# Attention scores in four array quarters, values loaded in wider runs, sums from the exponential, and a hint for a far branch

## The chip, the cores and the metric

The kernel runs on one core of a Trainium2 chip. The metric is the device time of one launch in microseconds; lower is better. One execution of each kernel is profiled as well. The engines are named as in the profile: PE is TensorE (PEld its weight loads), DVE VectorE, ACT ScalarE, POOL GpSimd, and SP the engine that issues most of the transfers. A `q` behind a name is that engine's sequencer.

## The reference

Three stages follow each other: attention over local windows plus block summaries, a mixture of eight experts with one expert per token, and a dense feed-forward layer with ELU.

```python
B, H, S, D = 2, 8, 768, 64
k_sum = k.reshape(B, H, nb, 32, D).max(axis=3)
v_sum = v.reshape(B, H, nb, 32, D).mean(axis=3)
scores_l = where(|i - j| < 16, scale * q @ k.T, -1e9)
scores_s = scale * q @ k_sum.T + log(32)
a = exp(scores_all - max);  a = a / (sum(a) + 1e-9)
x = a @ concat(v, v_sum)                          # (1536, 512) tokens
...
expert = argmax(x @ w_gate);  gate = softmax(...)[expert]
x = gate * (relu(x @ w1[expert]) @ w2[expert])    # 8 experts, 512 -> 1024 -> 512
...
h = x @ w_in;  out = elu(h) @ w_out               # 512 -> 2048 -> 512
```

## The kernel before

**Tiling of the attention.** The eight heads of a batch entry are taken as four pairs, so there are eight pairs in all. A pair holds 128 channels (two heads of 64) on the partitions. The 768 positions are 24 blocks of 32, of which two neighbouring ones make a query block of 64; a query block sees a window of 96 keys and 24 block summaries, 120 columns (`NK`). Four query blocks make a group; there are 24 groups, three for each pair.

**Steps of a group.** `scores(g)` (token `s:g`) multiplies queries by keys into a PSUM tile `sc` (L879): for each of the four query blocks two matmuls, one for each head, over all 128 partitions. So that a head's queries meet only its own keys, the query tile holds every head apart with zeros in the other head's rows; `zero_q` (L695, L696) writes these zeros and `queries` (L772) copies each head's rows. DVE then adds the mask and takes the row's extreme (L884, with a read of its accumulator after each of the four), and ACT takes the exponential (L888). `turn_weights(g)` (`t:g`) transposes the four tiles on PE into `pt` (L895), and ACT copies them to `pts` (L897). `average(g)` (`a:g`) multiplies by the values into `av` (L909), whose rows in SBUF carry a column of ones beside the values, so that one column of `av` is the sum of the weights; DVE adds 1e-9 (L915, twice), takes the reciprocal (L916) and scales into `xo` (L917).

**Other steps of a pair.** `load_k`, `load_q` and `load_v` (`lk`, `lq`, `lv`) issue loads on SP's queue. `key_sums` (`ks`, L807) takes the block maxima, `keys` (`kw`, L819 to L836) writes windows and summaries into one tile, and `sum_and_place_values` (`vq`, L855 to L860) forms the means of the values on PE, copies them on ACT and stores them into the value tile by a small transfer. `x_transpose` (`T`) and `x_store` (`X`) pass the finished tokens on to the routing.

**What sets the order.** The string `PROGRAM` lists these steps by hand; each engine executes its instructions in the order in which the steps issue them. Semaphores are placed by a tile framework: a PSUM pool with two buffers (`ps_a` for `sc`, `ps_b` for `av` and `pt`) makes a group wait for the group two before it.

**After the attention.** Everything from the routing on needs tokens of all groups: gather, five slots of 256 tokens, one wider slot, the dense layer. Behind the fifth slot an `If` (L1216, `extra`) holds spare slots which these inputs don't need; all engines branch over it. The wide slot's first layer (`hw`, L983 to L985, with ACT and DVE at L1160 and L1161) runs partly ahead of this branch and partly behind it.

Of the kernel before, what the change touches and what calls it, by code (L numbers as in the profile page):

```python
# [22 lines left out]
P = 128  # L23
# [9 lines left out]
VO = 2  # L33
VW = VO + 2 * D + VO
# [17 lines left out]
lq s:0 qp:0:v:1:3 zero:3 lv:0 ones:1 lk:1 lv:1 ks:1 vq:0:y  # L52
s:1 lv:2 kw:1:g:v lk:2 lk:3 t:0
s:2
s:3 t:1 a:0 t:2 zero:2
s:5 ks:2 vq:1:y kw:2 ones:3
s:4 a:1 a:2 t:5 t:3 ones:2 ks:3 lk:4 t:4 lv:3 vq:2:c kw:3 a:3
s:6
s:7 lv:4 a:4 a:5 t:6
s:8 t:7 consts lk:5  # L60
s:9 a:6 vq:3:c lv:5 t:8 T:1:0:c ks:4
s:10 kw:4 t:9
s:11 a:8 T:0:0 a:7 t:10 a:9 ks:5 lk:6 lv:6 t:11 T:0:1:c kw:5 ks:6 vq:4:c lk:7
# [50 lines left out]
def attention_moe_elu_kernel(  # L114
# [563 lines left out]
    pa = actx.enter_context(tc.tile_pool(name="ps_a", bufs=2, space=PSUM))  # L678

# [14 lines left out]
    def zero_q(n, eng):  # L694
        eng.memset(q_sb[n][D:P, :, 0, :], 0.0)  # L695
        eng.memset(q_sb[n][0:D, :, 1, :], 0.0)  # L696

    def ones_of(n):
        for col in (VO - 1, VO + 2 * D):
            nc.gpsimd.memset(v_sb[n][:NK, :, col], 1.0)  # L700

    def prep_consts():
        nc.scalar.activation(exps[:, 0, :], ident[:, 0:E], AF.Exp)
        zero_q(0, nc.vector)
        nc.gpsimd.memset(mask[:, :, 0:WIN], 0.0)
        nc.gpsimd.memset(mask[:, :, WIN:], 8.0 * LOG_BLOCK)
        for h in range(2):
            m = mask[h * D:(h + 1) * D, :, 0:WIN]
            for sgn in (1, -1):
                nc.gpsimd.affine_select(  # L710
                    out=m, in_=m, pattern=[[sgn * HALO, 3], [-sgn, WIN]], compare_op=ALU.is_ge,
                    fill=NEG, base=REACH, channel_multiplier=sgn,
                )
        nc.gpsimd.memset(sel, 0.0)
# [7 lines left out]
        ones_of(0)  # L722
# [62 lines left out]
    def load_v(n):  # L785
        if n >= B * NPAIR:
            return
        b, pr = divmod(n, NPAIR)
        sl = n % NQ
        vv = v_sb[sl][:, :, VO:VO + 2 * D]  # L790
        vb = v[b, :, pr * 2 * D:(pr + 1) * 2 * D]
        nc.sync.dma_start(
            out=vv[0:WIN, 1:NBLK - 1, :],
            in_=bass.AP(vb.tensor, vb.offset + win_start(1) * DM, [[DM, WIN], [QB * DM, NBLK - 2], [1, 2 * D]]),
# [3 lines left out]
            in_=bass.AP(vb.tensor, vb.offset, [[DM, WIN], [win_start(NBLK - 1) * DM, 2], [1, 2 * D]]),  # L798
# [71 lines left out]
    def scores(g):  # L870
        n, i0 = order[g]
        sl = n % NQ
        sc = pa.tile([P, 4, P], F32, tag="sc", name="sc")
        t = wk.tile([P, 4, NK], F32, tag="t", name="t", bufs=2)
        pe = wk.tile([P, 4, NK], F32, tag="pe", name="pe")
        nm = wk.tile([P, 4], F32, tag="nm", name="nm")
# [4 lines left out]
        for u in range(4):  # L881
            i = i0 + u
            kind = 0 if i == 0 else 2 if i == NBLK - 1 else 1
            nc.vector.tensor_tensor_reduce(  # L884
                out=t[:, u, :], in0=sc[:, u, :NK], in1=mask[:, kind, :], scale=-0.125, scalar=3.0e38,
                op0=ALU.add, op1=ALU.min, accum_out=nm[:, u:u + 1],
            )
            nc.scalar.activation(pe[:, u, :], t[:, u, :], AF.Exp, bias=nm[:, u:u + 1], scale=-1.0)  # L888
        st[g] = pe

    def turn_weights(g):
        pe = st[g]
        pt = pb.tile([P, 4, P], F32, tag="pt", name="pt")
        for u in range(4):
            nc.tensor.transpose(pt[:NK, u, :], pe[:, u, :], ident)  # L895
        pts = wk.tile([P, 4, P], F32, tag="pts", name="pts", bufs=2)
        nc.scalar.activation(pts[:NK], pt[:NK], AF.Copy)  # L897
        st[g] = pts

    def average(g):  # L900
        n, i0 = order[g]
        b, pr = divmod(n, NPAIR)
        pts = st.pop(g)
        av = pb.tile([P, 4, P], F32, tag="av", name="av")
        for u in range(4):
            for h in range(2):
                hs = slice(h * D, (h + 1) * D)
                col = VO - 1 + h * D
                nc.tensor.matmul(av[hs, u, :D + 2], pts[:NK, u, hs], v_sb[n % NQ][:NK, i0 + u, col:col + D + 2],  # L909
                                 start=True, stop=True)  # L910

        r = wk.tile([P, 4], F32, tag="r", name="r")
        for h in range(2):
            hs = slice(h * D, (h + 1) * D)
            nc.vector.tensor_scalar_add(r[hs], av[hs, :, h * (D + 1)], 1e-9)  # L915
        nc.vector.reciprocal(r, r)  # L916
        nc.vector.tensor_tensor(  # L917
            out=xo[b][:, i0:i0 + 4, pr, :], in0=av[:, :, 1:D + 1], in1=r.unsqueeze(2).to_broadcast([P, 4, D]),
            op=ALU.mult,
        )  # L920

    def x_transpose(ch, hf, e="c"):

        b, lo = divmod(4 * ch, NBLK)
        if ch not in xts:
            xts[ch] = rt2.tile([P, 2, 2, 4, QB], F32, tag="xts", name="xts")
        xt = pa.tile([P, 2, 4, QB], F32, tag="xt", name="xt")
        for bl in range(4):
            nc.tensor.transpose(
                xt[:, :, bl, :],  # L930
                xo[b][:, lo + bl, 2 * hf:2 * hf + 2, :].rearrange("p a d -> p (a d)"),
                ident,
            )
        copy[e](xts[ch][:, hf].rearrange("p a b q -> p a (b q)"), xt.rearrange("p a b q -> p a (b q)"))

    def x_store(ch):
        b, lo = divmod(4 * ch, NBLK)
        for par in range(2):
            nc.sync.dma_start(
                out=x_dram[4 * ch * QB:4 * (ch + 1) * QB, par * 256:(par + 1) * 256].rearrange(  # L940
                    "(i q) f -> q i f", q=QB),
                in_=xo[b][par * D:(par + 1) * D, lo:lo + 4].rearrange("q i a d -> q i (a d)"),
            )
# [109 lines left out]
    with tc.manual_schedule():  # L1053
# [6 lines left out]
        zero_q(1, nc.gpsimd)  # L1060
# [335 lines left out]
```

## Time and profile before

| | us |
|---|---|
| median of 3 runs | 549.58 |
| lowest to highest | 549.4 to 552.67 |
| profiled execution, its own time | 553.14 |
| its span, first to last instruction | 551.4 |
| PE busy in the span | 512.5 |
| DVE busy | 354.6 |
| ACT busy | 238.2 |
| POOL busy | 168.7 |

The span leaves 1.74 us of the profiled execution outside. Durations and waits below come from this one execution, which was 3.56 us above the median of the runs. A busy engine is not yet a bound: shares are averages over stages with different limits.

### The profile page before, as it was taken

To read this page: it belongs to the slowest core of one execution; us is meant where nothing else is said; L and a number is where in the kernel's file an instruction comes from. 1 tells how busy PE (TensorE), PEld (TensorE's weight loads), DVE (VectorE), ACT (ScalarE), POOL (GpSimd) and SP (SyncE) were. 2 spreads that over 40 slices of the span, in tenths; PEclk is the share of its full clock that TensorE was granted. 3 is DMA by queue.
4 is the path that set the end of the run, shared out by engine and by line. 5 is a ranking of instruction groups with operands and counts; after the bars stand their busy time and mean duration, and the time that the engine had idled before them with its cause. 6 is when DMAs were issued, how large, how long until landed. Compare 5 with 4: busy or idle time off the path is not lost.

```text
span 551.4 us, 9535 instructions
## 1 busy us (share of the span) xinstructions
PE 512.5 (93%) x3605; PEld 443.1 (80%) x3605; DVE 354.6 (64%) x820; ACT 238.2 (43%) x444; POOL 168.7 (31%) x164
## 2 busy tenths in 40 slices
PE   6798998889999996979987999999999999999995
PEld 4686786779999996979965888888888888888884
DVE  5766788868869785538998778774334354434342
ACT  3644567434555545433444434353323243323231
POOL 6556504633345373503345224322000001100002
PEclk7987999989999999889999999999999999999999
DMA  8788726746666577752545434101000000100001
GB/s 199 205 179 224 172 35 231 226 151 215 223 214 181 203 260 224 226 159 76 162 144 153 114 85 134 51 0 58 19 0 1 0 1 38 40 1 1 0 1 76
DMA packets 34999, 64.56 MB, mean 117 GB/s; under 512 B 3136, under 2 KB 18112, under 8 KB 34944
## 3 DMA queue, kind: packets, MB, share of 16 engines
q1 hardware_dynamic: 31384, 56.57, 35.1%
q0 software_dynamic: 2000, 6.56, 3.3%
q10 hardware_dynamic: 1560, 0.74, 0.9%
q8 instruction: 31, 0.51, 0.4%
q14 instruction: 24, 0.20, 0.1%
HBM read 56.38 MB, written 6.29 MB: 114 GB/s over the span
## 4 chain that ended last, share of the span: by engine, by line
PE 47%; DVE 6%; issue 2%; POOL 1%; POOLq 0%; ACT 0%; DVEq 0%
PE o L985 7%; PE o L983 7%; PE o L984 7%; PE hp L984 7%; PE hp L983 7%; PE hp L985 7%; DVE v L215 2%; PE hw L983 1%; PE hw L985 1%; PE hw L984 1%; DVE v L212 1%; DVE raw L218 1%; DVE x L212 1%; POOL out_dram L1313 1%; DVE h_lo L1037 0%
## 5 line engine op out<-in xcount | busy, mean ns | idle before, releaser
L1271 DVE SCALAR_TENSOR_TENSOR xs<-xs,xs 128x512 f32<-128x512 f32 x48 | 33.2, 691 | 82.0 <-ACT xs L1268 82.0
L984 PE MATMUL hp<-h_lo,whi 128*128 128x512 f32 x192 | 75.1, 391 | 0.0
L983 PE MATMUL hp<-h_hi,whi 128*128 128x512 f32 x192 | 75.0, 391 | 0.0
L985 PE MATMUL hp<-h_hi,wlo 128*128 128x512 f32 x192 | 75.0, 390 | 0.0
L224 POOL TENSOR_TENSOR wlo<-raw,whi 128x512 fp32r<-128x512 f32 x32 | 45.4, 1425 | 96.5 <-ACT whi L223 96.5
L983 PE MATMUL o<-whi,x_hi 128*128 128x512 f32 x168 | 65.8, 391 | 1.7 <-ACT x_hi L1282 1.7
L985 PE MATMUL o<-whi,x_lo 128*128 128x512 f32 x168 | 65.8, 392 | 0.9 <-DVE x_lo L1284 0.9
L1267 ACT ACTIVATE xs<-hp 128x512 f32<-128x512 f32 x48 | 28.6, 596 | 87.9 <-PE hp L985 87.9
L984 PE MATMUL o<-wlo,x_hi 128*128 128x512 f32 x168 | 65.7, 391 | 0.0
L1313 POOL DMA_INDIRECT out_dram<-x,idx_cmp x12 | 11.6, 968 | 172.6 <-DVE x L1312 156.7
L296 ACT ACTIVATE whi<-raw 128x1024 fp32r<-128x1024 f32 x46 | 48.0, 1054 | 24.5 <-DMA raw<-in_w_dram 24.1
L299 DVE TENSOR_TENSOR wlo<-raw,whi 128x1024 fp32r<-128x1024 f32 x32 | 43.9, 1379 | 19.1 <-ACT whi L296 19.0
L983 PE MATMUL hp<-x_hi,whi 128*128 128x256 f32 x160 | 47.0, 294 | 4.0 <-DVE h_lo L1003 3.9
L1282 ACT ACTIVATE x_hi<-xs 128x512 fp32r<-128x512 f32 x42 | 26.6, 632 | 54.2 <-DVE xs L1273 54.2
L299 POOL TENSOR_TENSOR wlo<-raw,whi 128x1024 fp32r<-128x1024 f32 x14 | 35.5, 2538 | 47.3 <-ACT whi L296 47.3
L984 PE MATMUL yp<-h_lo,whi 128*128 128x256 f32 x160 | 46.3, 290 | 2.3 <-DVE h_lo L1003 2.2
L1284 DVE TENSOR_TENSOR x_lo<-xs,x_hi 128x512 fp32r<-128x512 f32 x40 | 30.3, 758 | 28.1 <-ACT x_hi L1282 27.3
L984 PE MATMUL hp<-x_lo,whi 128*128 128x256 f32 x160 | 46.5, 291 | 1.1 <-DVE x_lo L979 1.1
L985 PE MATMUL yp<-h_hi,wlo 128*128 128x256 f32 x160 | 46.1, 288 | 0.7 <-DVE wlo L299 0.7
L983 PE MATMUL yp<-h_hi,whi 128*128 128x256 f32 x160 | 46.8, 292 | 0.0
L985 PE MATMUL hp<-x_hi,wlo 128*128 128x256 f32 x160 | 46.3, 289 | 0.0
L983 PEld LDWEIGHTS hp<-h_hi,whi 128*128 128x128 f32 x192 | 36.0, 188 | 7.9
(252 smaller groups left out, 1184.1 us busy)
## 6 DMA issues: line engine op xcount, KB each, us to landing
raw<-in_w_dram SPq DMA_DIRECT2D x48, 512.0 KB, 4.6
raw<-in_win_dram SPq DMA_DIRECT2D x16, 512.0 KB, 4.1
raw<-in_wout_dram SPq DMA_DIRECT2D x16, 512.0 KB, 3.7
v<-in_v_dram SPq DMA_DIRECT2D x8, 480.0 KB, 6.9
x_dram<-xo SPq DMA_DIRECT2D x12, 256.0 KB, 4.9
kr<-in_kT_dram SPq DMA_DIRECT2D x7, 384.0 KB, 3.8
qr<-in_qT_dram SPq DMA_DIRECT2D x7, 384.0 KB, 4.3
v<-in_v_dram SPq DMA_DIRECT2D x8, 96.0 KB
```

Source lines behind the costliest of these rows:

```text
L212: nc.vector.tensor_scalar(out=v, in0=top, scalar1=3, scalar2=0x3FFFFFF8, op0=ALU.logical_shift_left, op1=ALU.bitwise_and)
L224: nc.gpsimd.tensor_tensor(out=wlo[n][:, k, :], in0=w, in1=as_f32(whi[n][:, k, :]), op=ALU.subtract)
L296: nc.scalar.activation(part, raw, AF.Copy)
L299: eng_.tensor_tensor(out=wlo[n][:, k, :], in0=raw, in1=as_f32(part), op=ALU.subtract)
L983: nc.tensor.matmul(o, a_hi, b_hi, start=first, stop=False)
L984: nc.tensor.matmul(o, a_hi, b_lo, start=False, stop=False)
L985: nc.tensor.matmul(o, a_lo, b_hi, start=False, stop=last)
L1267: nc.scalar.activation(u, hp, AF.Exp)
L1271: nc.vector.scalar_tensor_tensor(out=u, in0=u, scalar=1.0, in1=t, op0=ALU.add, op1=ALU.mult)
L1282: nc.scalar.activation(gh, g, AF.Copy)
L1284: (nc.gpsimd if twice else nc.vector).tensor_tensor(out=gl, in0=g, in1=as_f32(gh), op=ALU.subtract)
L1313: puts.append(nc.gpsimd.indirect_dma_start(out=out[:, :], out_offset=bass.IndirectOffsetOnAxis(ap=idx_cmp[:, 4 * blk + t:4 * blk + t + 1], ...
```

## The change

- **Scores.** The query tile has no zeros. Each matmul takes 64 partitions (one head) into 64 output partitions (one query block of 64), and four of them, one after the other, address the four quarters of the array: head 0 into the upper half, head 1 into the lower, then crosswise. Two neighbouring query blocks lie side by side on the partitions, and the two heads in two different banks.
- **PSUM.** The score tile is one tile `sc` of three banks by two sides, allocated once; a group takes the halves `2*(g % 3)` and the next. `av` is one tile of one bank with two sides.
- **Values.** Two pairs' values share one tile. Pairs 0 and 1 are loaded apart; from pair 2 on one load brings two pairs, in runs of 1 KB (512 bytes before). The tokens `lv:3`, `lv:5` and `lv:7` are gone, `lv:4` and `lv:6` stand elsewhere. The columns of ones are gone.
- **Sums.** The exponential on ACT writes the row's sum through its accumulator; DVE adds 1e-9 once.
- **Stores.** `x_store` issues one transfer for each chunk, not two.
- **Hint.** The branch over the spare slots has a prefetch hint, "likely taken", on all five engines.

```diff
@@ PROGRAM
-lq s:0 qp:0:v:1:3 zero:3 lv:0 ones:1 lk:1 lv:1 ks:1 vq:0:y
+lq s:0 qp:0:v:1:3 lv:0 lk:1 lv:1 ks:1 vq:0:y
...
-s:4 a:1 a:2 t:5 t:3 ones:2 ks:3 lk:4 t:4 lv:3 vq:2:c kw:3 a:3
+s:4 a:1 a:2 t:5 t:3 ks:3 lk:4 t:4 vq:2:c kw:3 a:3
@@ PSUM
+    av_of = ...tile_pool(name="ps_v", bufs=1, space=PSUM)).tile([P, 2, 2, 2, D], F32, name="av")
...
+    sc_of = psc.tile([P, 3, 2, 2, P], F32, name="sc")
@@ load_v
+        w = 2 * D if n < 2 else 4 * D
+        vv = values(n) if n < 2 else v_sb[n // 2 % (NQ // 2)]
@@ scores
-        for u in range(4):
-            for h in range(2):
-                nc.tensor.matmul(sc[h * D:(h + 1) * D, u, :NK], q_sb[sl][:, i0 // 4, h, u * QB:(u + 1) * QB],
-                                 k_sb[sl][:, i0 + u, :], start=True, stop=True)
+        half_of = [divmod(2 * (g % 3) + h, 3) for h in range(2)]
+        sc = [sc_of[:, bank, side] for side, bank in half_of]
...
+        for u in range(2):
+            for p, h in ((0, 0), (1, 1), (1, 0), (0, 1)):
+                i, hs = i0 + 2 * u + p, slice(h * D, (h + 1) * D)
+                nc.tensor.matmul(sc[h][p * QB:(p + 1) * QB, u, :NK], q_sb[sl][hs, i, :], k_sb[sl][hs, i, :],
+                                 start=True, stop=True)
...
-            nc.scalar.activation(pe[:, u, :], t[:, u, :], AF.Exp, bias=nm[:, u:u + 1], scale=-1.0)
+                nc.scalar.activation(pe[:, u, h, :], t[:, u, h, :], AF.Exp, bias=nm[:, u, h:h + 1], scale=-1.0,
+                                     accum_out=sums[:, u, h:h + 1])
@@ average
-        av = pb.tile([P, 4, P], F32, tag="av", name="av")
+        av = av_of[:, g % 2]
...
-        for h in range(2):
-            hs = slice(h * D, (h + 1) * D)
-            nc.vector.tensor_scalar_add(r[hs], av[hs, :, h * (D + 1)], 1e-9)
+        nc.vector.tensor_scalar_add(r, sums, 1e-9)
@@ around the spare slots
+                if j + 1 == SURE:
+                    tc.mark_branch_hint_location("spare", hint="LikelyTaken", engines=[...])
...
-                with tc.If(nslots > j):
+                with tc.If(nslots > j, label="spare" if j == SURE else None):
```

The first place is PE from the scores of group 5 to the transposes after `a:2`, with the semaphores on which each row waits (the number behind a name tells one buffer of a tile from another). Before:

```order
L879 MATMUL sc_394<-k1_132,q1_128 64x120 [waits DVE_49,PE_49]
L879 MATMUL sc_394<-k1_132,q1_128 64x120 x7
L855 MATMUL pv_416<-v1_136,sel_142 64x128 [waits DMAHW1_49]
L855 MATMUL pv_416<-v1_136,sel_142 64x128 [waits DMAHW0_49]
L855 MATMUL pv_416<-v1_136,sel_142 64x128 x10
L879 MATMUL sc_440<-k1_132,q1_128 64x120 [waits DVE_49,PE_49]
L879 MATMUL sc_440<-k1_132,q1_128 64x120 x7
L909 MATMUL av_460<-v0_135,pts_369 64x66 [waits Activation_49]
L909 MATMUL av_460<-v0_135,pts_369 64x66 x7
L909 MATMUL av_474<-v0_135,pts_390 64x66 [waits DVE_49,Activation_49]
L909 MATMUL av_474<-v0_135,pts_390 64x66 x7
L895 MATMUL pt_488<-ident_61,pe_396 120x128 [waits Activation_49] x4
```

The same place on PE after the change:

```order
L881 MATMUL sc_122<-k1_140,q1_136 64x120 [waits DVE_49]
L881 MATMUL sc_122<-k1_140,q1_136 64x120 x7
L852 MATMUL pv_407<-v0_143,sel_148 64x128 [waits DMAHW1_49]
L852 MATMUL pv_407<-v0_143,sel_148 64x128 [waits DMAHW0_49]
L852 MATMUL pv_407<-v0_143,sel_148 64x128 x10
L881 MATMUL sc_122<-k1_140,q1_136 64x120 [waits DVE_49]
L881 MATMUL sc_122<-k1_140,q1_136 64x120 x7
L915 MATMUL av_118<-v0_143,pts_364 64x64 [waits Activation_49]
L915 MATMUL av_118<-v0_143,pts_364 64x64 x7
L915 MATMUL av_118<-v0_143,pts_383 64x64 [waits DVE_49,Activation_49]
L915 MATMUL av_118<-v0_143,pts_383 64x64 x7
L900 MATMUL pt_472<-ident_61,pe_387 120x128 [waits PE_49,Activation_49]
```

The order is the same, but all scores write one tile, `sc_122`, and all averages one tile, `av_118`. The value of DVE's semaphore for which a row waits is not printed above: the scores of group 4 (second `sc`) wait for DVE's fourth read of the accumulator of group 5, which stands just before them, where they waited for a group further back; and the second average, `a:2`, waits for DVE's `xo` of `a:1`, where it waited for the `xo` of `a:0`.

The second place is SP, the queue of loads, from the loads of pair 1's values on. Before:

```order
L792 DMA v1_136<-in_v_dram 96x10x128 [waits DMAHW0_49]
L796 DMA v1_136<-in_v_dram 96x2x128 [waits DMAHW1_49]
L860 DMA v0_135<-vs_278 12x12x128 [waits DMAHW2_49,Activation_49]
L860 DMA v0_135<-vs_278 12x12x128 [waits DMAHW3_49]
L792 DMA v2_137<-in_v_dram 96x10x128 [waits DMAHW4_49]
L796 DMA v2_137<-in_v_dram 96x2x128 [waits DMAHW5_49]
L781 DMA kr_309<-in_kT_dram 128x768 [waits DMAHW6_49,DVE_49,Pool_49]
L764 DMA qr_311<-in_qT_dram 128x768 [waits DMAHW7_49]
```

The same place on SP after the change:

```order
L789 DMA v0_143<-in_v_dram 96x10x128 [waits DMAHW0_49]
L793 DMA v0_143<-in_v_dram 96x2x128 [waits DMAHW1_49]
L857 DMA v0_143<-vs_274 12x12x128 [waits DMAHW2_49,Activation_49]
L857 DMA v0_143<-vs_274 12x12x128 [waits DMAHW3_49]
L789 DMA v1_144<-in_v_dram 96x10x256 [waits DMAHW4_49]
L793 DMA v1_144<-in_v_dram 96x2x256 [waits DMAHW5_49]
L779 DMA kr_304<-in_kT_dram 128x768 [waits DMAHW6_49,DVE_49,Pool_49]
L764 DMA qr_306<-in_qT_dram 128x768 [waits DMAHW7_49]
```

The load `lv:2` brings twice the bytes ahead of the keys and queries of pair 2, which stand behind it on the same queue.

The third place is the start of the kernel on PE, after the change:

```order
L1400 UNCONDITIONAL_BRANCH [waits barrier_Pool_Activation_PE_DVE_SP_release]
L1400 BRANCH_PREFETCH_HINT
L1053 LDWEIGHTS const-bfloat16-1.0
L1053 MATMUL wu_182<-const-bfloat16-1.0 128x512
L1053 LDWEIGHTS const-bfloat16-1.0
```

The hint stands as the first instruction behind the entry on PE, and on the other four engines as well, though its mark in the code stands near the end of the fifth slot; before, the warm-up matmuls follow the entry directly.

## Rows read from the trace of the kernel before

**Rows 1.** Stretches: length; busy (count) of PE, PEld, DVE, ACT, POOL; clock; DMA; GB/s.

```profile
12.40:50.00 37.60, 31.80 (x470) 27.15 (x468) 26.27 (x137) 21.30 (x62) 20.17 (x34) 0.91 0.83 201
50.00:91.60 41.60, 39.43 (x601) 32.45 (x600) 31.86 (x192) 24.01 (x70) 17.16 (x17) 0.94 0.60 156
50.00:55.00 5.00, 5.00 (x46) 4.28 (x49) 1.60 (x4) 0.88 (x2) 4.63 (x6) 0.50 0.72 203
85.00:90.00 5.00, 4.64 (x76) 3.75 (x74) 4.75 (x32) 4.15 (x12) 3.26 (x3) 1.00 0.99 363
```

**Rows 2.** Groups of instructions, 0 to 100 us: busy us, mean ns, idle before.

```profile
L888 ACT ACTIVATE pe<-t,nm 128x120 f32<-128x120 f32 x96 | 29.7, 383 | 24.8 <-DVE nm L884 23.1 <-DVE r L916 1.7
L879 PE MATMUL sc<-k,q 128*64 128x120 f32 x384 | 26.8, 288 | 3.1 <-DVE k L825 2.3 <-DVE k L819 0.8
...
L897 ACT ACTIVATE pts<-pt 120x512 f32<-120x512 f32 x24 | 13.6, 582 | 8.4 <-PE av L909 4.3 <-PE pt L895 2.4 <-PE sc L879 1.7
...
L884 DVE DVE_READ_ACCUMULATOR2_ANT nm<- 128x1 f32 x96 | 7.9, 83 | 0.1
L915 DVE TENSOR_SCALAR r<-av 64x4 f32<-64x4 f32 x48 | 7.5, 157 | 3.9 <-PE av L909 3.2
```

**Rows 3.** Timeline of PE, 19.3 to 27.5 us: start, length, idle before.

```profile
21.55 0.99 PE L879 MATMUL sc<-k,q 128*64 128x120 f32 x16
22.38 1.11 PE L909 MATMUL av<-v,pts 120*64 120x66 f32 x32
23.41 1.09 PE L895 MATMUL pt<-ident,pe 128*120 128x128 f32 x8
26.63 0.65 PE L895 MATMUL pt<-ident,pe 128*120 128x128 f32 x4 [2.13 <-ACT pts L897]
```

**Rows 4.** Timeline of DVE over the same stretch.

```profile
23.09 0.95 DVE L807 TENSOR_REDUCE ksum<-kr 128x24 f32<-128x768 f32 x1 [1.62 <-DMA kr<-in_kT_dram]
23.96 0.65 DVE L819 COPY k<-kr 128x960 f32<-128x960 f32 x1
...
25.91 0.42 DVE L917 TENSOR_TENSOR xo<-av,r 128x256 f32<-128x256 f32 x1
```

**Rows 5.** Timeline of PE, 34.5 to 38.5 us.

```profile
34.98 1.04 PE L879 MATMUL sc<-k,q 128*64 128x120 f32 x16
35.95 0.65 PE L895 MATMUL pt<-ident,pe 128*120 128x128 f32 x4
```

**Rows 6.** Timeline of DVE, 34.5 to 38.5 us.

```profile
36.17 0.28 DVE L884 CUSTOM_DVE_ANT_0 t<-sc,mask 128x120 f32<-128x120 f32 x1 [0.79 <-PE sc L879]
...
36.99 0.08 DVE L884 DVE_READ_ACCUMULATOR2_ANT nm<- 128x1 f32 x1
```

**Rows 7.** Transfers, 0 to 30 us: GB/s in 40 slices of 0.75 us.

```profile
GB/s 0 0 72 340 290 167 173 241 215 183 245 262 332 369 216 204 178 140 45 37 86 90 146 299 237 252 258 325 352 389 393 228 88 99 44 167 360 377 261 169
```

**Rows 8.** Instructions of L1216, the branch: ns; first and last start.

```profile
L1216 PEldq COMPARE_BRANCH  x1: 3483/3483/3483, 237.7 to 237.7; - x1
...
L1216 DVEq COMPARE_BRANCH  x1: 72/72/72, 239.5 to 239.5; - x1
...
L1216 DVEq EVENT_SEMAPHORE  x1: 21/21/21, 243.3 to 243.3; - x1
```

**Rows 9.** Timeline of PE around the branch.

```profile
240.03 0.32 PE L984 MATMUL hw<-wlo,whi 128*128 128x344 f32 x1
240.19 0.32 PE L985 MATMUL hw<-whi,wlo 128*128 128x344 f32 x1
243.45 0.63 PE L983 MATMUL hw<-whi,whi 128*128 128x344 f32 x1 [2.95 <-DVEq L1216]
...
244.16 0.49 PE L985 MATMUL hw<-whi,wlo 128*128 128x344 f32 x1
244.45 0.49 PE L983 MATMUL hw<-whi,whi 128*128 128x344 f32 x1
```

**Rows 10.** Chain that ended last, 258 to 260 us: start, length, work.

```profile
258.49 0.47 ACT wlo L1160
```

More of the change, by code (lines that the diff above doesn't have):

```diff
@@ L897, in turn_weights @@
+        st[g] = pe, sums
+    def turn_weights(g):
+        pe, sums = st[g]
+        pt = pb.tile([P, 2, 2, P], F32, tag="pt", name="pt")
+        for u in range(2):
+            for h in range(2):
+                nc.tensor.transpose(pt[:NK, u, h, :], pe[:, u, h, :], ident)
+        pts = wk.tile([P, 2, 2, P], F32, tag="pts", name="pts", bufs=2)
         nc.scalar.activation(pts[:NK], pt[:NK], AF.Copy)
-        st[g] = pts
+        st[g] = pts, sums
     def average(g):
@@ L902, in average @@
         b, pr = divmod(n, NPAIR)
-        pts = st.pop(g)
-        av = pb.tile([P, 4, P], F32, tag="av", name="av")
-        for u in range(4):
+        pts, sums = st.pop(g)
+        vv = values(n)
+        av = av_of[:, g % 2]
+        for u in range(2):
             for h in range(2):
-                hs = slice(h * D, (h + 1) * D)
-                col = VO - 1 + h * D
-                nc.tensor.matmul(av[hs, u, :D + 2], pts[:NK, u, hs], v_sb[n % NQ][:NK, i0 + u, col:col + D + 2],
-                                 start=True, stop=True)
@@ L912, in average @@
-        r = wk.tile([P, 4], F32, tag="r", name="r")
-        for h in range(2):
-            hs = slice(h * D, (h + 1) * D)
-            nc.vector.tensor_scalar_add(r[hs], av[hs, :, h * (D + 1)], 1e-9)
+                for p in range(2):
+                    ps_ = slice(p * QB, (p + 1) * QB)
+                    nc.tensor.matmul(av[ps_, u, h, :], pts[:NK, u, h, ps_],
+                                     vv[:NK, i0 + 2 * u + p, h * D:(h + 1) * D], start=True, stop=True)
+        r = wk.tile([P, 2, 2], F32, tag="r", name="r")
@@ L925, in x_transpose @@
         if ch not in xts:
[L926 to L934, printed above, removed]
-    def x_store(ch):
[L937 to L943, printed above, removed]
+            xts[ch] = rt2.tile([P, 2, 2, 2 * P], F32, tag="xts", name="xts")
@@ new lines, in x_transpose @@
+        xt = pa.tile([P, 2, 2, P], F32, tag="xt", name="xt")
+        for k in range(2):
+            for par in range(2):
+                nc.tensor.transpose(
+                    xt[:, par, k, :],
+                    xo[b][:, lo + k, par, 2 * hf:2 * hf + 2, :].rearrange("p a d -> p (a d)"),
+                    ident,
+                )
+        copy[e](xts[ch][:, hf], xt.rearrange("p a k q -> p a (k q)"))
+    def x_store(ch):
+        b, lo = divmod(2 * ch, HT)
+        nc.sync.dma_start(
+            out=x_dram[2 * ch * P:2 * (ch + 1) * P, :].rearrange("(k p) f -> p k f", p=P),
+            in_=xo[b][:, lo:lo + 2].rearrange("p k h a d -> p k (h a d)"),
+        )
```

107 lines of the change are left out of this document (49 added, 58 removed).

## The prediction

> **What bounds the kernel now.** I read the stretches of the attention first [rows 1]. From 12.4 to 50 us PE is busy 31.80 of 37.60 us, so 5.8 us of idle time lie there; from 50 to 91.6 us it is busy 39.43 of 41.60 us. The first half is therefore a pipeline in which PE repeatedly waits for others, the second half is close to PE's own work, with DVE near its limit at the end (4.75 of 5.00 us from 85 to 90). This decides what a shorter score is worth: in the second half it can shorten the stage, in the first half it must get past a wait. Everything behind the attention needs tokens of all groups, so what the stage wins or loses by 92 us passes on. Then I read the groups of instructions [rows 2] for the sizes, the timelines of PE and DVE around the longest idle time [rows 3, 4] for which wait ends last, and the branch at L1216 [rows 8 to 10], which no other part of the change touches.
>
> **Scores in quarters.** 384 score matmuls stay 384 [rows 2]. A group's 16 rows (eight loads, eight matmuls) occupy PE from 21.55 to 22.38 = 0.83 us where averages follow [rows 3], and from 34.98 to 35.95 = 0.97 us where transposes follow [rows 5]. After the change four quarters can work at once where two halves did. The nearest row is the average, with the same 16 rows and about half the columns: two groups take 22.38 to 23.41, 0.52 us each [rows 3]. I take 0.52 for the score, a saving of 0.31 us a group; the bounds are none at all (if the quarters in the lower and upper rows don't overlap) and half of 0.83, 0.42. For 24 groups that is 7.4 us of PE's work, from 0 to 10.
>
> What of it reaches the end: twelve groups lie ahead of 50 us, and there the chain through DVE described below sets the time, so I count nothing for them. Of the twelve behind 50 us the last four run beside a DVE that is full [rows 1] and give nothing; eight give 8 x 0.31 = 2.5 us.
>
> A rule speaks against this part, and the sum doesn't use it. The row first: a score followed by transposes holds PE 0.14 us longer than one followed by averages [rows 3, 5]. The Trainium skill, page "TensorEngine Tiling (Array Packing)", section "Key Properties", says that a change of the tiling mode drains the array. By it the quartered scores would differ in mode from the averages and value means as well, and eight groups would lose up to 8 x 0.14 = 1.1 of the 2.5 us; the sum would be 547.3 in place of 546.2.
>
> **One buffer where there were two.** Since `sc` is now one tile, the scores of a group wait for DVE's last read of the group before. That takes, from the end of a score at 35.95 to the start of the fourth accumulator read at 36.99 plus its 0.08, 1.12 us [rows 5, 6]. Where an average, transposes or value means stand between two scores, most of it is covered by them. Where scores follow each other directly (groups 2 and 3, 6 and 7, 20 and 19) it isn't. The first two pairs lie ahead of a wait that is longer anyway; the third, in the full second half, costs 1.12 less some DVE start already overlapped, 0.9 us.
>
> `av` is one tile too, so `a:2` waits for the `xo` of `a:1`. Before, `a:1` and `a:2` ran back to back at 22.38, and PE then stood for 2.13 us until 26.63, when ACT's copies let `t:4` begin [rows 3]. On DVE that `xo` stands behind the key sums of pair 2, which waited 1.62 us for their transfer and began at 23.09, behind the copy at 23.96 and the four reductions of `s:4`: it ends at 25.91 + 0.42 = 26.33 [rows 4]. So `a:2` and the transposes `t:5` and `t:3` behind it move from inside the idle time to its end.
>
> **Wider values.** `lv:2` now stands with 1152 KB in place of 576 KB ahead of those keys. The transfer view shows 237 to 258 GB/s in the slices of the values' 512-byte runs and 352 to 393 in those of the keys' 3 KB rows [rows 7]. With one fixed price for a run and one for a byte, 1 KB runs come to about 305 GB/s (an estimate from these two): 1180 kB in 3.9 us against 590 kB at 245 in 2.4, so the keys come 1.45 us later; at 245 it would be 2.4, at 390 it would be 0.6. Later loads of values have slack; the two loads saved and the joined stores run on SP, which nobody waits for, and cost nothing as long as the keys stay ahead of need; if not, the price is that of the keys above.
>
> **The sum at t:4.** The `xo` of `a:1` ends at 26.33 + 1.45 - 0.16 (one addition of 157 ns less on DVE [rows 2]) = 27.6. Then `a:2` takes 0.52 and `t:5` half of 1.09 [rows 3]; ACT copies `t:5` out (0.58 [rows 2]), and `t:4` gets its buffer at 29.25, 2.6 us later than 26.63. With the keys' bounds it is 1.8 to 3.6. The remaining idle time ahead of 50 us, 5.8 less 2.13, takes back some; these gaps are waits for ACT and DVE that move with the chain, so I count only 0.6. That leaves +2.0.
>
> **Sums on ACT and DVE.** The 96 exponentials (383 ns each [rows 2]) get an accumulator. No row shows its price on ACT; the nearest is DVE's read of an accumulator, 83 ns [rows 2]. It lies between nothing (ACT's pipeline hides it) and, generously, three times that; I take 0.1 us, 0.4 a group. ACT is busy 21.30 of 37.60 us ahead of 50 [rows 1], and PE waits for it in a few places only: I count one group, +0.4. DVE loses 24 of its 48 additions of 157 ns [rows 2], 3.8 us in all, none of it where DVE sets the end except the 0.16 used above. The zeros, ones and the split query copies that go were done by POOL and DVE ahead of need; the first groups start a little earlier and then meet the transfer of keys, so they count nothing.
>
> **The hint.** PE's branch stands 3483 ns, DVE's is at 239.5 and its next event only at 243.3 [rows 8]. PE's last matmul ahead begins at 240.19, the next at 243.45, idle for 2.95 us until DVE's sequencer had passed the branch [rows 9]. After that the matmuls come every 0.29 us, not 0.16: PE had idled and its clock was granted at the 1.2 GHz level for about ten matmuls, 10 x 0.13 = 1.3 us. The stretch is on the chain that ended last, since the `hw` matmuls behind it release ACT's L1160 at 258.49 [rows 10]. If all engines find their code ready, 2.95 + 1.3 = 4.2 us go. If the hint does nothing, the branch stays as it is.
>
> As built, the hint is the first instruction of the kernel, some 235 us ahead of the branch. The row shows the cost of a jump into code that isn't there. The Trainium skill, page "Runtime: NRT & Kernel Launch", section "Instruction fetch mechanics", says that instructions are prefetched only in sequence and that a taken branch out of the window forces a fetch. The trace agrees with the stall; that a hint can change it no run here shows, and by the rule alone the time would be the first rival's.
>
> **Sum.** Attention +2.0 (t:4) +0.4 (ACT) +0.9 (scores 20 and 19) -2.5 (scores) = +0.8; hint -4.2; together -3.4. The profiled execution of 553.14 would take 549.7. It was 3.56 above the median, so from the median of 549.58 I get **546.2 us**. About 1%, 5.5 us, is what a measurement can tell from no change.
>
> **Rivals.**
> - *The hint does nothing* that far ahead: +0.8 alone, **550.4**. For it: the distance, and 3483 ns that a fetch takes. Against it: the branch is named in the hint, and nothing in the trace says that it is forgotten.
> - *The quarters pass through.* If PE sets the time in the first half too, because the earlier scores let DVE start earlier and the wait of `a:2` disappears in the 5.8 us of idle time, all 7.4 us count, less 1.4 for the direct pairs and ACT: -6, and with the hint -10.2, **539.4** (543.6 without). For it: PE is the busiest engine. Against it: the 2.13 us at 26.63 end with a chain that starts with a transfer.
> - *Slower: the single buffers lock PE to DVE.* Place: `a:1`/`a:2`, and behind 50 us every score with less than 1.1 us of other PE work since the score before. Price: +3.6 at t:4, six groups there at half of 1.12 = 3.4, ACT at its upper bound 0.9, and 1.3 us at the 1.2 GHz level after a longer wait (a stretch at 0.50 followed a wait before [rows 1]), less 2.5: +6.7, with an idle hint **556.3**. It decides when the saving of 0.31 a group is smaller than what the waits uncover.
>
> **Chances.** Forecast 0.39 (its own range 543.5 to 549), no hint 0.25 (548 to 553), quarters pass 0.21 (537 to 544), locked 0.15 (552 to 559). The range of 8 in 10 leaves out the lower third of the third case and most of the last: 538.5 to 555. Faster than 544.1: nearly all of the quarters' case and a little of the forecast, 0.27. Slower than 555.1: most of the last, with a little of no hint, 0.13. Within 1%: 0.60.
>
> **What would show it.** In the changed profile: score matmuls issued in about 0.5 us a group; PE idle ahead of `a:2` with DVE's `xo` as releaser, and `t:4` some 2.6 us later than 26.63; key sums of pair 2 near 24.5; exponentials spaced wider by 0.1; at the `If`, no idle of 3 us and no run of 0.29 us spacing. The forecast falls if the branch still costs 3.5 us, if scores still take 0.8, or if `a:2` runs on without waiting.

## The result and the profile after

The changed kernel takes 559.24 us (median of 4 runs, 556.76 to 560.71) against 551.12 for the kernel before, measured again beside it (549.4 to 552.74): a ratio of 1.0126 with a 95% interval of 1.0091 to 1.016. It is slower by about 6.9 us. The forecast was 546.2 with a range up to 555. The profiled execution took 559.96 us, its span is 558.3. Here and below a time is the median of all runs of a kernel, while a ratio and its interval leave out the few slow runs, those more than 1.5% above the fastest of the same kernel.

First the stretches of the attention after the change (columns as in [rows 1]).

```profile
12.40:50.00 37.60, 26.17 (x426) 20.45 (x424) 20.67 (x114) 20.65 (x89) 10.93 (x24) 0.86 0.65 167
50.00:91.60 41.60, 33.57 (x539) 25.06 (x540) 30.24 (x169) 27.02 (x115) 8.70 (x13) 0.97 0.56 156
30.00:35.00 5.00, 5.00 (x48) 4.30 (x50) 2.35 (x6) 1.19 (x2) 2.62 (x6) 0.59 0.17 63
```

PE is busy 26.17 of 37.60 us where it was 31.80, and 33.57 of 41.60 us where it was 39.43 [rows 1]. PE's idle time grew in both halves, from 5.8 to 11.4 us and from 2.2 to 8.0. From 30 to 35 us PE is busy all the time at a granted clock of 0.59, the 1.2 GHz level for most of the stretch.

The groups of instructions of the first 108 us (busy us, mean ns, idle before and its releasers), the answer to [rows 2]:

```profile
L891 ACT ACTIVATE pe<-t,nm 128x120 f32<-128x120 f32 x96 | 36.6, 384 | 22.2 <-DVE nm L887 18.2 <-DVE mc L442 2.1 <-DVE lgs L344 1.7
...
L891 ACT ACTIVATION_READ_ACCUMULATOR pe<-t,nm 128x1 f32 x96 | 18.2, 189 | 0.0
L915 PE MATMUL av<-v,pts 120*64 120x64 f32 x384 | 17.7, 239 | 13.7 <-DVE r L918 6.0 <-DVE xo L920 4.6 <-ACT pts L902 1.9
L881 PE MATMUL sc<-k,q 64*64 64x120 f32 x384 | 16.4, 289 | 8.2 <-DVE nm L887 5.9 <-DVE k L822 1.6 <-DVE wg_sb L725 0.7
```

The scores' PE time falls from 26.8 to 16.4 us. The exponential has brought a second instruction, a read of the accumulator of 189 ns, 96 times, 18.2 us; about half of it overlaps the exponentials, which now start 0.38 us apart (16.96 after 16.58) where four in a row took 1.25 us, (1.25 - 0.38) / 3 = 0.29 apart. And the averages, ahead of which PE idled 2.3 us in all before, now stand 6.0 us for DVE's `r` and 4.6 us for DVE's `xo`. Their row before (0 to 100 us):

```profile
L909 PE MATMUL av<-v,pts 120*64 120x66 f32 x384 | 16.2, 230 | 2.3 <-ACT pts L897 1.7 <-DVE nm L884 0.5 <-DVE xo L917 0.2
```

The timeline of PE at the first place, the answer to [rows 3]:

```profile
22.59 0.64 PE L881 MATMUL sc<-k,q 64*64 64x120 f32 x16
23.16 0.69 PE L915 MATMUL av<-v,pts 120*64 120x64 f32 x16
29.87 1.12 PE L915 MATMUL av<-v,pts 120*64 120x64 f32 x16 [6.03 <-DVE r L918]
30.92 2.90 PE L900 MATMUL pt<-ident,pe 128*120 128x128 f32 x12
33.76 1.67 PE L852 MATMUL pv<-v,sel 96*64 96x128 f32 x24
...
35.83 0.43 PE L881 MATMUL sc<-k,q 64*64 64x120 f32 x7
```

And DVE over the same time, the answer to [rows 4]:

```profile
25.66 0.95 DVE L804 TENSOR_REDUCE ksum<-kr 128x24 f32<-128x768 f32 x1 [3.36 <-DMA kr<-in_kT_dram]
26.53 0.65 DVE L816 COPY k<-kr 128x960 f32<-128x960 f32 x1
...
27.90 1.08 DVE L918 TENSOR_SCALAR r<-sums 128x4 f32<-128x4 f32 x1
...
29.30 0.43 DVE L920 TENSOR_TENSOR xo<-av,r 128x256 f32<-128x256 f32 x1
```

Read from below: `a:2` begins at 29.87, after 6.03 us of idle time, when DVE has finished the `xo` of `a:1` (29.30 + 0.43; the profile names the `r` that follows it, which doesn't touch `av`). That `xo` stands behind an `r` of 1.08 us, four reductions, the copy of keys at 26.53 and the key sums at 25.66, which waited for their transfer. Then the twelve transposes take 2.90 us, where eight took 1.09 [rows 3], with the clock at the lower level after the long wait. The scores of group 6 begin at 35.83; before they began at 30.02. The delay of 5.8 us shrinks to 2.7 at the scores of group 13 (58.73 against 56.06), where the kernel before had its own stretch at the lower clock [rows 1], and grows again: the last scores begin at 94.97 against 86.61, and the first `hw` matmul ahead of the branch at 247.96 against 238.43, 9.5 us later.

The branch, the answer to [rows 8] (ns; first and last start) and, below it, to [rows 9] on PE's timeline:

```profile
L1224 PEldq COMPARE_BRANCH  x1: 786/786/786, 247.3 to 247.3; - x1
...
L1224 DVEq COMPARE_BRANCH  x1: 84/84/84, 249.0 to 249.0; - x1
L1224 DVEq EVENT_SEMAPHORE  x1: 21/21/21, 249.6 to 249.6; - x1
```

```profile
249.72 0.32 PE L987 MATMUL hw<-whi,wlo 128*128 128x344 f32 x1
250.34 0.40 PE L985 MATMUL hw<-whi,whi 128*128 128x344 f32 x1 [0.30 <-PEq L1224]
250.57 0.32 PE L986 MATMUL hw<-wlo,whi 128*128 128x344 f32 x1
250.73 0.32 PE L987 MATMUL hw<-whi,wlo 128*128 128x344 f32 x1
```

PE's branch takes 786 ns instead of 3483, DVE passes it in 0.6 us instead of 3.8, the idle time falls from 2.95 to 0.30 us, and the matmuls behind it come every 0.16 us at once. ACT's `wlo` that ends this stretch begins at 264.04, 5.55 us later than before, after 9.5 us at the first `hw`: 4.0 us were won here.

### The profile page after: what moved, and what is told of

The parts are those of the page before. It is cut to its first block, busy times and chain, and to the rows that moved or that the text cites. A ratio compares the mean times of both kernels' runs of the same rounds, so it can differ in the third digit from the quotient of the medians.

```text
span 558.3 us, 9596 instructions
## 1 busy us (share of the span) xinstructions
PE 506.8 (91%) x3605; PEld 432.9 (78%) x3605; DVE 352.9 (63%) x792; ACT 246.3 (44%) x540; POOL 152.5 (27%) x145
## 4 chain that ended last, share of the span: by engine, by line
PE 46%; DVE 6%; issue 2%; POOL 1%; POOLq 0%; ACT 0%; DVEq 0%
PE o L987 7%; PE o L986 7%; PE o L985 7%; PE hp L986 7%; PE hp L985 7%; PE hp L987 7%; DVE v L213 2%; PE hw L985 1%; PE hw L987 1%; DVE v L210 1%; PE hw L986 1%; DVE raw L216 1%; POOL out_dram L1321 1%; DVE x L210 1%; DVE h_lo L1039 0%
## 5 line engine op out<-in xcount | busy, mean ns | idle before, releaser
L297 DVE TENSOR_TENSOR wlo<-raw,whi 128x1024 fp32r<-128x1024 f32 x32 | 45.0, 1413 | 18.6 <-ACT whi L294 18.2
L891 ACT ACTIVATE pe<-t,nm 128x120 f32<-128x120 f32 x96 | 36.6, 384 | 22.2 <-DVE nm L887 18.2
```

The source lines that it names most:

```text
L297: eng_.tensor_tensor(out=wlo[n][:, k, :], in0=raw, in1=as_f32(part), op=ALU.subtract)
L891: nc.scalar.activation(pe[:, u, h, :], t[:, u, h, :], AF.Exp, bias=nm[:, u, h:h + 1], scale=-1.0, accum_out=sums[:, u, h:h + 1])
```

## The experiments

Each ratio is to the kernel before on the same chip in the same rounds; its own runs scatter by about 1% there (547.27 to 554.33 in one set), so an interval is some 0.4% to either side, 2 us, and twice that for experiments 3 and 6, with four runs each.

**1. The kernel before with the hint alone.**

```diff
+                if j + 1 == SURE:
+                    tc.mark_branch_hint_location("spare", hint="LikelyTaken", engines=[...])
...
-                with tc.If(nslots > j):
+                with tc.If(nslots > j, label="spare" if j == SURE else None):
```

> The kernel before with the branch hint alone. Theory: the hint works from the start of the kernel; PE's idle time of 2.95 us at the If and the ten matmuls at the 1.2 GHz level go, 3 to 4 us less than before (about 547 to 548). Rival: the shorter branch in the changed kernel has to do with its other timing, and the hint alone changes nothing (within 1 us).

546.92 us, ratio 0.9934 (0.9889 to 0.9979): 3.6 us faster. The branch in its trace (columns as above) and PE behind it:

```profile
L1220 PEldq COMPARE_BRANCH  x1: 501/501/501, 232.2 to 232.2; - x1
```

```profile
235.31 0.40 PE L983 MATMUL hw<-whi,whi 128*128 128x344 f32 x1 [0.30 <-PEq L1220]
```

The hint works, also where nothing else is changed. From the first `hw` matmul to ACT's `wlo` it is 16.09 us here (232.93 to 249.02), 16.08 in the changed kernel and 20.06 before. So the rest of the change costs about 1.0126 / 0.9934 = 1.019, some 10.5 us, which the hint partly hid.

**2. Keys ahead of the wide load of values.**

```diff
-s:1 lv:2 kw:1:g:v lk:2 lk:3 t:0
+s:1 kw:1:g:v lk:2 lk:3 lv:2 t:0
```

> The changed kernel with the loads of keys and queries of pairs 2 and 3 issued ahead of the 1152 KB of values. Theory: the late keys start the largest loss; key sums of pair 2 begin near 20 to 21 us instead of 25.66, the idle time of 6.03 us ahead of a:2 falls to 2 or less, the 1.2 GHz stretch after it goes, and the kernel is 4 to 6 us faster than the changed one. Rival: the waits for the shared score tile and ACT's reads of accumulators make the loss all along the stage, so that what is won here is lost again by 90 us; within 1.5 us of the changed kernel.

553.99 us, ratio 1.0056 (1.0019 to 1.0092), nearly 4 us below the changed kernel's 1.0126. The key sums begin at 23.14 and no longer wait for their transfer, though not before 21 as I had written; the wait of `a:2` falls to 2.19 us. But now the values come late:

```profile
27.35 0.69 PE L915 MATMUL av<-v,pts 120*64 120x64 f32 x16 [2.19 <-DVE r L918]
...
31.20 1.53 PE L852 MATMUL pv<-v,sel 96*64 96x128 f32 x24 [1.25 <-DMA v<-in_v_dram]
```

The order of the two loads moves part of the wait from the keys to the values, which points to the bytes as the cost; experiment 8 tests that.

**3. No sums of the weights.** The exponential has no accumulator, and a constant stands for the sums, so the weights aren't normalized.

```diff
-        sums = wk.tile([P, 2, 2], F32, tag="sums", name="sums", bufs=6)
+        sums = sums1
...
-... AF.Exp, bias=nm[:, u, h:h + 1], scale=-1.0, accum_out=sums[:, u, h:h + 1])
+... AF.Exp, bias=nm[:, u, h:h + 1], scale=-1.0)
```

> The changed kernel without the sums of the weights: the exponential has no accumulator, and the weights are divided by a constant instead. Theory: 96 reads of ACT's accumulator at 189 ns (each spacing the exponentials 0.09 wider) cost some 2 us in the second half of the attention, where ACT's copies end PE's waits; 1.5 to 3 us faster than the changed kernel. Rival: they hide in ACT's idle time; within 1 us.

557.1 us, ratio 1.0108 (1.0027 to 1.0189); against 1.0126 nothing that can be told from no difference. PE's wait ahead of `a:2` is still 6.43 us. But the interval is 4 us to either side, so it doesn't tell the theory's 1.5 to 3 us from nothing either.

**4. Two tiles for the averages.** The scores' tile shrinks to two banks, which changes none of its waits.

```diff
-    av_of = ...tile_pool(name="ps_v", bufs=1, space=PSUM)).tile([P, 2, 2, 2, D], F32, name="av")
-    sc_of = psc.tile([P, 3, 2, 2, P], F32, name="sc")
+    sc_of = psc.tile([P, 2, 2, 2, P], F32, name="sc")
...
-        sc = [sc_of[:, bank, side] for side, bank in half_of]
+        sc = [sc_of[:, h, g % 2] for h in range(2)]
...
-        av = av_of[:, g % 2]
+        av = pb.tile([P, 2, 2, D], F32, tag="av", name="av")
```

> The changed kernel with two tiles for the averages in two banks, so that an average waits for the one two groups before, as in the kernel before; the scores' tile gets two banks and keeps its wait for the group just before. Theory: a:2 runs at once behind a:1, but t:4 still waits for the late keys through DVE and ACT; 1 to 3 us faster than the changed kernel, most of it from the waits for xo behind 80 us. Rival: the wait of the averages is the largest loss; 5 us or more.

550.36 us, ratio 0.9989 (0.9947 to 1.0032): 7.5 us below the changed kernel. That is beyond my 1 to 3 us; the rival was right, the wait of the averages is the largest loss.

**5. Both: two averages and keys first.**

> The changed kernel with both edits, two tiles for the averages and the keys of pairs 2 and 3 ahead of the wide load of values. If the late keys and the wait of a:2 are two links of one chain, the gains overlap in part, and the ratio to the kernel before is 0.985 to 0.992; if they are separate losses the gains add up (4 and 7 us) and it is 0.98 or less; if two tiles alone had already taken the chain away, keys first gives nothing more, 0.996 or above.

552.96 us, ratio 1.0004 (0.9959 to 1.0048): keys first adds nothing to two averages. PE's timeline shows why:

```profile
27.36 0.65 PE L898 MATMUL pt<-ident,pe 128*120 128x128 f32 x4 [0.84 <-ACT pts L900]
31.08 2.83 PE L851 MATMUL pv<-v,sel 96*64 96x128 f32 x24 [3.08 <-DMA v<-in_v_dram]
```

PE reaches the value means of pair 2 early and waits 3.08 us for the 1152 KB.

**6. The kernel before with one buffer for the averages.**

```diff
-        av = pb.tile([P, 4, P], F32, tag="av", name="av")
+        av = pb.tile([P, 4, P], F32, tag="av", name="av", bufs=1)
```

> The kernel before with one buffer for the averages, nothing else. Theory: the wait of an average for the xo of the group just before is the largest loss of the change even without late keys: 3 to 6 us slower than before. Rival: it costs only together with the late keys: under 1.5 us slower.

559.89 us, ratio 1.0121 (1.0041 to 1.0201): 6.7 us slower from this alone (the interval is 2 to 11 us), where the theory had 3 to 6. In the groups of instructions PE's idle time ahead of the averages is 10.6 us, 6.0 of it for DVE's `xo`, and on its timeline both direct pairs, `a:1`/`a:2` and `a:4`/`a:5`, stand apart:

```profile
L909 PE MATMUL av<-v,pts 120*64 120x66 f32 x368 | 16.0, 230 | 10.6 <-DVE xo L917 6.0 <-issue 2.2 <-DMA v<-vs 1.1
```

```profile
23.26 0.63 PE L909 MATMUL av<-v,pts 120*64 120x66 f32 x16
26.56 0.69 PE L909 MATMUL av<-v,pts 120*64 120x66 f32 x16 [2.67 <-DVE xo L917]
...
33.81 0.63 PE L909 MATMUL av<-v,pts 120*64 120x66 f32 x16
36.09 0.69 PE L909 MATMUL av<-v,pts 120*64 120x66 f32 x16 [1.65 <-DVE xo L917]
```

**7. The kernel before with one buffer for the scores.**

```diff
+    psc = sctx.enter_context(tc.tile_pool(name="ps_s", bufs=1, space=PSUM))
...
-        sc = pa.tile([P, 4, P], F32, tag="sc", name="sc")
+        sc = psc.tile([P, 4, P], F32, tag="sc", name="sc")
```

> The kernel before with one buffer for the scores, nothing else. Theory: only the groups whose scores follow each other directly lose some 1.1 us each, half of it in idle time that is there anyway: 1 to 3 us slower. Rival: all groups are locked to DVE: 5 us or more.

552.22 us, ratio 0.998 (0.9944 to 1.0017): no difference, less than either theory had. The waits themselves are in its trace, 1.20 us for DVE's `nm` ahead of the scores of groups 7 and 19; the whole time doesn't show them.

**8. The kernel before with the values of pair 3 early.**

```diff
-s:1 lv:2 kw:1:g:v lk:2 lk:3 t:0
+s:1 lv:2 lv:3 kw:1:g:v lk:2 lk:3 t:0
...
-s:4 a:1 a:2 t:5 t:3 ones:2 ks:3 lk:4 t:4 lv:3 vq:2:c kw:3 a:3
+s:4 a:1 a:2 t:5 t:3 ones:2 ks:3 lk:4 t:4 vq:2:c kw:3 a:3
```

> The kernel before with the values of pair 3 loaded right behind those of pair 2, ahead of the keys of pairs 2 and 3, in 512-byte runs as before: the bytes ahead of the keys are those of the changed kernel. Theory: the key sums of pair 2 begin some 2.4 us later and t:4 with them, 2 to 3 us slower than before. Rival: with two buffers for averages the pipeline absorbs it: within 1 us.

557.74 us, ratio 1.0093 (1.0055 to 1.013): 5.1 us slower, twice what I had written for the theory. On DVE, PE, and in the stretch behind (columns as in [rows 1]):

```profile
25.46 0.95 DVE L807 TENSOR_REDUCE ksum<-kr 128x24 f32<-128x768 f32 x1 [2.97 <-DMA kr<-in_kT_dram]
```

```profile
29.00 1.11 PE L895 MATMUL pt<-ident,pe 128*120 128x128 f32 x4 [3.48 <-ACT pts L897]
30.04 2.83 PE L855 MATMUL pv<-v,sel 96*64 96x128 f32 x24
```

```profile
30.00:35.00 5.00, 5.00 (x65) 4.96 (x66) 1.96 (x6) 0.77 (x2) 4.82 (x9) 0.58 0.91 201
```

The key sums come 2.4 us later and so does `t:4` (29.00 against 26.63), as expected; but the wait of PE grows to 3.48 us and the stretch from 30 to 35 us runs at a granted clock of 0.58. The value means of pair 2, which took 1.53 us in the trace of experiment 2 and 2.14 in that of the kernel before, take 2.83 here, and the scores of group 6 begin at 33.53 against 30.02, 3.5 us later. So the slow stretch adds about 1 us to the 2.4; where the rest of the 5.1 us is lost these two traces don't tell.

**9. Two averages, and values pair by pair up to pair 3.** On top of experiment 4:

```diff
-        w = 2 * D if n < 2 else 4 * D
+        w = 2 * D if n < 4 else 4 * D
...
-... t:4 vq:2:c kw:3 a:3
+... t:4 lv:3 vq:2:c kw:3 a:3
```

> The changed kernel with two tiles for the averages, and with the values of pairs 0 to 3 loaded pair by pair at their old places in the order (512-byte runs; later pairs in 1 KB runs). Nothing then delays keys or values. Theory: late keys and the wait of a:2 were the whole loss of the attention beside ACT's accumulators; ratio to the kernel before 0.985 to 0.993, about the hint's 0.9934 or better by what the quartered scores bring. Rival: the one score tile and ACT's reads still cost more than the quarters bring; 0.996 to 1.003.

548.6 us, ratio 0.9934 (0.9893 to 0.9975): 3 us below experiment 4, faster than both kernels, and just what the hint alone gives. With the two losses undone the attention costs, within 2 us, what it cost before, although what else the change does (the order of tokens in `xo`, the joined stores, another PSUM pool for the first slot) is still in this kernel. The idle time ahead of its averages is gone:

```profile
L913 PE MATMUL av<-v,pts 120*64 120x64 f32 x384 | 16.8, 235 | 0.6 <-DVE r L916 0.5 <-ACT pts L900 0.2
```

**10. The same without the sums of the weights** (a constant in their place, as in experiment 3).

> The same kernel without the sums of the weights (no accumulator on the exponential, a constant in place of the sums). Theory: with the other waits gone ACT's 96 reads of accumulators stand on the path in the second half; 2 to 4 us faster than the same kernel with them. Rival: within 1 us.

545.21 us, ratio 0.9887 (0.9833 to 0.9941). The middle lies 2.6 us below experiment 9, but the intervals overlap: it points to the theory without settling it.

**11. The kernel of experiment 9 with other work between the scores.**

```diff
-s:2
-s:3 t:1 a:0 t:2
+s:2 t:1
+s:3 a:0 t:2
...
-s:6
-s:7 a:4 a:5 lv:4 t:6
+s:6 a:4
+s:7 a:5 lv:4 t:6
...
-s:20
-s:19 t:18 E:choose E:places:v a:17
+s:20 t:18
+s:19 E:choose E:places:v a:17
```

> The same kernel as the one with two averages and narrow loads, sums included, with a transposing or averaging step set between the scores of groups 2 and 3, 6 and 7, and 20 and 19. Theory: each pair wins up to 0.6 us of a wait of 1.2 us, 0.5 to 1.5 us in all. Rival: nothing, as the single score buffer of the kernel before cost nothing.

548.49 us, ratio 0.9943 (0.9911 to 0.9974): nothing, the rival.

**12. Quartered scores in one tile, with values, averages and sums as before, and the hint.** Values pair by pair with columns of ones, averages of 66 columns in two tiles, sums from PE:

```diff
-                                     accum_out=sums[:, u, h:h + 1])
...
-                                     vv[:NK, i0 + 2 * u + p, h * D:(h + 1) * D], start=True, stop=True)
+                                     v_sb[n % NQ][:NK, i0 + 2 * u + p, col:col + D + 2], start=True, stop=True)
...
-        nc.vector.tensor_scalar_add(r, sums, 1e-9)
+        for h in range(2):
+            nc.vector.tensor_scalar_add(r[:, :, h], av[:, :, h, h * (D + 1)], 1e-9)
```

> The kernel before with the quartered scores, their one score tile in two banks, the joined stores and the hint; averages in two tiles, values pair by pair with columns of ones, sums from PE and nothing added on ACT, as before. Theory: the quartered scores are worth about 2.5 us once nothing else is changed; ratio 0.986 to 0.991, below the hint's 0.9934 and close to the kernel that leaves out the sums. Rival: the quarters bring nothing, since DVE and ACT set the pace; 0.992 to 0.997.

546.85 us, ratio 0.9915 (0.9878 to 0.9951), also faster than both kernels. The middle is 1 us below the hint alone, inside the intervals: what the quarters bring is between nothing and some 3 us, and these runs don't fix it.

## Why the prediction was wrong

**The hint: right.** 4.2 us were forecast; 4.0 were won at the place, and 3.6 by the ratio of experiment 1. A hint as the kernel's first instruction was enough. The rule cited there, from the Trainium skill's page "Runtime: NRT & Kernel Launch", section "Instruction fetch mechanics", would have left the stall; for a hinted branch the measurement decides against it.

**Scores in quarters: right in size, not in effect.** A score that averages follow holds PE from 22.59 to 23.16, 0.57 us, where 0.52 was taken and 0.83 measured before; one that transposes follow holds it as long (41.39 to 41.96). That doesn't decide on the rule of the Trainium skill's page "TensorEngine Tiling (Array Packing)", section "Key Properties": by it the quarters differ in mode from both neighbours, and a price that is the same with both would not show. What the shorter score is worth in the second half can be read from a stretch that is alike in every execution of the same attention, from the start of the scores of group 13 to that of group 23 on PE's timelines (one execution each; granted clock 1.00, in the last two rows 0.93 to 0.95):

| | us |
|---|---|
| before; the same attention in experiments 1 and 8 | 30.55; 30.72, 30.71 |
| before with one buffer for the scores (7) | 32.78 |
| quarters in one score tile, the rest as before (12) | 31.49 |
| the changed kernel with two averages and narrow values (9, 11) | 33.18, 32.83 |
| the same without sums on ACT (10) | 32.28 |
| before with one buffer for the averages (6) | 34.25 |
| the changed kernel; with keys first (2) | 36.24; 36.76 |

The quarters give 1.3 us there (12 against 7), and the score tile that comes with them takes 2.2 (7), where I had -2.5 and +0.9. How much of these small terms reaches the end the whole times don't tell; experiment 7's shows none of its 2.2.

**The step that failed: "one buffer where there were two".** I counted the averages' single tile at one place, `a:2`, and none in the second half, where I counted only the scores 20 and 19, 0.9 us. The runs show the reverse. One score buffer costs nothing that can be measured in the whole time (experiment 7; 11 agrees), and one average buffer costs 6.7 us by itself (6), 7.5 in the changed kernel (4), of which 3.7 and some 3 lie between the scores of groups 13 and 23 (6 against before, the changed kernel against 9). In the second half DVE does routing work for later steps between the attention's own. An average that waits for the `xo` before it waits for all that DVE has in between. In the changed kernel's timeline, `a:17`'s `xo` stands behind a row of routing operations on DVE, and PE waits for it ahead of `a:18`:

```profile
84.62 0.20 DVE L449 TENSOR_TENSOR mine<-oh,st 128x48 f32<-128x48 f16 x1
...
86.36 1.05 DVE L420 TENSOR_SCALAR bm<-iota_p,r 128x128 f16<-128x128 f16 x6
...
87.81 0.42 DVE L920 TENSOR_TENSOR xo<-av,r 128x256 f32<-128x256 f32 x1
```

```profile
88.33 0.84 PE L915 MATMUL av<-v,pts 120*64 120x64 f32 x16 [2.03 <-DVE xo L920]
```

The operation `L420` alone takes 1.05 us, the `xo` comes at 87.81, the average at 88.33 after 2.03 us. Nearly all that the averages' single tile costs in the second half lies here. From `a:17` to the scores of group 22, before, after, and in experiment 6:

```profile
79.32 0.69 PE L909 MATMUL av<-v,pts 120*64 120x66 f32 x16
84.13 1.02 PE L879 MATMUL sc<-k,q 128*64 128x120 f32 x16
```

```profile
84.15 0.69 PE L915 MATMUL av<-v,pts 120*64 120x64 f32 x16
92.32 0.64 PE L881 MATMUL sc<-k,q 64*64 64x120 f32 x16
```

```profile
81.06 0.69 PE L909 MATMUL av<-v,pts 120*64 120x66 f32 x16
89.24 0.99 PE L879 MATMUL sc<-k,q 128*64 128x120 f32 x16
```

That is 4.81 us before, 8.17 after and 8.18 with one average buffer alone; in experiment 9, with two, it is 5.27. The wait is 2 us of it, and behind it PE's clock falls (granted 0.79 from 90 to 95 us in the changed kernel, 1.00 before). I had named DVE full there (4.75 of 5.00 us) and drawn from it only that a shorter score gives nothing. It also says that a new wait for DVE costs most there. This is the third rival's mechanism, at its place `a:1`/`a:2`; behind 50 us that rival spoke of scores, and it was averages.

**The sum at t:4: mechanism right, three terms too small.** Forecast were +2.6 there and +2.0 kept; the scores of group 6 came 5.8 us later. ACT's copy of `t:5`, for which `t:4` waits, ended at 32.67, so `t:4` came some 6 us after 26.63:

```profile
32.07 0.60 ACT L902 ACTIVATE pts<-pt 120x512 f32<-120x512 f32 x1 [3.04 <-PE pt L900]
```

First, the keys came 2.57 us later (25.66 against 23.09), not 1.45: the estimate that 1 KB runs go faster doesn't hold. In the slices of 0.75 us of the changed kernel,

```profile
GB/s 0 0 76 287 253 150 248 238 211 209 255 259 322 371 203 201 210 148 31 20 68 94 185 223 299 225 239 232 258 247 321 377 397 406 289 128 41 90 252 367
```

the values move at 223 to 299 GB/s, like the 512-byte runs [rows 7]; and in experiment 8, with the same bytes in 512-byte runs, the key sums begin no later, at 25.46. My upper bound of 2.4 was close. Second, DVE: the forecast took 0.16 us off for the addition that goes, but the one that is left took 1.08, so the `xo` ended at 29.73 and not at 27.6, 1.0 us more beside the 1.1 of the keys. Third, the clock, which stood only in the slower rival, at 1.3 us: PE stood 6.03 us, ran at the lower level behind it (0.59 from 30 to 35 us), and from the `xo` to `t:4` took 2.9 us where I had added up 1.6. With the 2.6 forecast, 1.1 + 1.0 + 1.3 make up the 6 us.

The profile that the forecast rests on also had a wait of its own at this place. In experiment 1, with the same attention, `t:4` hardly waits, the clock stays at 1.00 from 25 to 35 us (0.80 and 0.86 in the profile before), and the scores of group 6 begin at 28.00, not 30.02:

```profile
25.59 0.65 PE L895 MATMUL pt<-ident,pe 128*120 128x128 f32 x4 [0.48 <-ACT pts L897]
```

So the 2.13 us of idle time ahead of `t:4`, which were to hide part of the new waits, belonged to that execution and not to the kernel (0.31 us in experiment 7).

The averages' wait and the late keys cost 6.7 and 5.1 us alone in the kernel before (6 and 8); taken out of the changed kernel one after the other they give back 7.5 and then 3 (4 and 9), together the 10.5 us that the change without its hint loses. Whether they share a part or add up, these intervals don't tell.

**Sums on ACT.** I took 0.1 us for an exponential. The instruction added is 189 ns, of which the spacing of two exponentials shows a part, 0.38 against 0.29. That fits the size; the effect, forecast as 0.4 in all, is 0 to 3 us and not settled by the whole times (3 and 10). Between the scores of groups 13 and 23 it is about 0.9 us without the averages' wait (33.18 against 32.28) and 1.8 with it (36.24 against 34.46 in experiment 3).

**What stays open:** how much of the quarters and of the accumulators reaches the end of the kernel, each being smaller than the scatter of these runs; and whether the single tile or the PSUM bank makes two turns wait as one. Both sides of `av` lie in one bank, and two groups that follow each other share a bank of `sc`; no run gives the turns of one tile banks of their own.

## What to carry to other kernels

A tile that is allocated once and indexed by turns can be one buffer for whoever places the waits, as both were here, so count buffers by what each instruction waits for, not by the shape of the tile. Before a double buffer is given up, look at everything that the other engine does between producer and consumer: where it is nearly full and runs work for other steps, a wait for it costs that work too. Price a wait that makes PE stand for some microseconds together with the slow stretch behind it.

## What was not expected of the hardware

- A prefetch hint given as the first instruction of a kernel still held for a branch some 235 us later, across everything executed in between (PE's branch 3483 ns without, 786 and 501 with it).
- Transfers in runs of 1 KB were no faster than in 512 bytes beside the same neighbours (223 to 299 GB/s against 237 to 299), while runs of 3 KB reached about 390.
- The accumulator of ACT's exponential is read by an instruction of its own (189 ns), as DVE's is (83 ns).
- DVE's addition `r<-sums` at 27.90 took 1.08 us, where the median of the 24 is 0.16. POOL's copy `q<-qr` ran from 27.41 for 1.55 us, and both end at 28.97 within 0.02. It is no accident of one execution: in all eight traces with `r<-sums` (the changed kernel, experiments 2 to 5 and 9 to 11) this `r` takes 0.56 to 1.42 us and ends 0.02 to 0.04 us after POOL's copy, and in experiment 12, whose `r` reads `av`, the two together take 0.22 us in the middle of the copy. That DVE waits for POOL there fits them all; no run takes the copy away.
